# Running sums in the result's PSUM bank: a change to the seven-product steps of an attention and MLP kernel

## The chip, the cores and the metric

The kernel runs on one core of one Trainium2 chip. The metric is the device time of one execution in microseconds (us); lower is better. Three runs of the kernel before took 652.58, 654.79 and 655.5 us, median 654.79 us.

## The reference

A lightning attention (4 batches, 8 heads, 768 positions, head size 64) gives a token matrix `x` of 3072 x 512. An MLP follows:

```python
h = x @ w_in             # 3072x512 @ 512x2048
g = h - np.tanh(h)
return g @ w_out         # 3072x2048 @ 2048x512
```

The attention goes over blocks of positions with a running state per head (`kv_state`); scores inside a block are masked by powers of `lam`.

## The kernel before, in words

The tokens are worked off in six groups `g` = 0 to 5 of 512 tokens (128 positions of each batch). Each group passes attention, "up" (`x @ w_in` and the tanh step) and "down" (`g @ w_out`). Both products use Strassen's scheme in Winograd's form: a 2 x 2 block product is made of seven products P1 to P7 instead of eight, and sums of blocks are formed before and after. Groups 2 to 5 use the scheme on two levels: each of the seven outer products `n` is itself made of seven inner products `x`. On the inner level the results are, with P for the inner products:

- c11 = P1 + P2
- c12 = P1 + P6 + P5 + P3
- c21 = P1 + P6 + P7 + P4 (the signs are in the operands)
- c22 = P1 + P6 + P7 + P5

So three running sums are wanted, P1, P1 + P6 and P1 + P6 + P7. TensorE makes them in one place, `y`: P1 starts it, P6, P7 and P4 are added to it, and after each of them ScalarE copies the state of `y` away (line 819). P2 and P3 go to `zw`, where VectorE later picks them up.

`down_twice(g, n)` (from line 801) is an inner round of "down". Its inner product is 128 x 128, of four matrix products over the 2048 hidden units; each of the four appears in the trace as two passes, so an inner product is eight passes of TensorE. There are 32 calls: 5 in group 1 (n = 4, 5, 6, 7, 3), 7 in each of groups 2 to 4, and 6 in group 5. Each is a generator that hands control back after each inner product, and `steps` and `every` drive it. `y` is a part of one bank of PSUM (128 columns of 512), `zw` is a whole bank with P2, P3 and P5 in three quarters of it. VectorE adds P5 and P2 (lines 828 and 829), and then combines the outer products (lines 832 to 844). The rounds for n = 1 are woven into "up", those for n = 3 into `inner_steps`; all others (n = 2, 4, 5, 6, 7) run with their seven inner products one after the other.

`inner_steps(g, n)` (from line 627) is the same for "up" with n = 1, 2, 5, 6. Here two rounds run in turn, `pa` with `pb` (and with `down_twice` for n = 3 between them), then `pc` with `pd`. Each inner product is 128 x 512, of four products to four quarters of a bank.

`sums_twice` (lines 791 to 799) forms the sums of blocks that P5, P6, P7 and P3 read (`s1`, `s2`, `s3`, `s4`) on VectorE; for n > 2 `s4` is `a12 - s2`, in place of `a12`, once P2 has read `a12` (line 821). `sums_once` (line 743) forms operands of the outer level.

The weight blocks come from HBM through `send` on GpSimd's queue (line 700), seven ahead of their use (`RING`); the order of `stream` decides which is fetched first. `SUB` is the order in which they lie in HBM, `STEPS` that of their use.

PSUM has eight banks: `ya`, `yb`, `z`, `w` are single ones, `att` is a ring of four. A tile framework puts in the semaphores, one counter for each engine; it also orders instructions where `tied` and `keep_in_program_order` leave it free to.

After "down" n = 2 and after n = 6 comes `att_out` of the next group, small matrix products for the attention, whose results ScalarE copies to `xt` (line 484).

Of the kernel before, what the change touches and what calls it, by code (L numbers as in the profile page):

```python
# [15 lines left out]
AF = mybir.ActivationFunctionType  # L16
AL = mybir.AluOpType
# [7 lines left out]
def kernel(  # L25
# [32 lines left out]
    nc = tc.nc  # L58
# [6 lines left out]
    NG = S // BLK  # L65
    HB = GRP // 2
    NU = DFF // 512
# [61 lines left out]
    def tied(yes, op):  # L129
        return tc.keep_in_program_order(op) if yes else op  # L130
# [81 lines left out]
    SUB = (1, 2, 6, 5, 7, 3, 4)  # L212
    GI = 2
# [408 lines left out]
                nc.vector.tensor_tensor(dst, x, y, op=AL.subtract)  # L622
            toks[g, n] = {1: b11, 2: b21, 3: b22, 4: t4, 5: t1, 6: t2, 7: b12}

    STEPS = (1, 2, 6, 5, 7, 3, 4)

    def inner_steps(g, n):

        tags = {1: ("yb", "att", "att"), 2: ("w", "att", "att"), 5: ("ya", "att", "z"), 6: ("yb", "att", "att")}[n]
        y, w, z = (bank(x, tag, 4 if tag == "att" else 1) for x, tag in zip(("y3", "w3", "z3"), tags))  # L630
        r5 = otile("r5")
        out4 = hidden(g, {1: 12, 2: 11, 5: 22, 6: 21}[n])
        c11, c12, c21, c22 = (out4[:, :, i, ts(j, 128)] for i in range(2) for j in range(2))
        for x in STEPS:
            b = toks[g, n][x]
            wb = piece(g, ("in", n), x) if x in (3, 5, 6) else None
            dst = w if x == 2 else z if x in (3, 5) else y
            for u in range(NU):
                a = wb.rearrange("p m c -> p (m c)")[:, ts(u, 128)] if wb is not None else a_quarter(
                    n, u, *{1: (0, 0), 2: (0, 1), 7: (1, 0), 4: (1, 1)}[x])  # L640
                nc.tensor.matmul(out=dst[:, ts(u, 128)], lhsT=a, rhs=b, start=x in (1, 2, 5) and u == 0, stop=True,  # L641
                                 skip_group_check=True)
            d = dst.rearrange("q (u c) -> q u c", u=NU)
            if x in (1, 4, 6):
                op = tied(False, nc.scalar.activation({1: c11, 4: c21, 6: c12}[x], d, AF.Copy))  # L645
                if (n, x) == (1, 6) and g < NG - 1:
                    hold[g + 1] = op
                    load((g + 1) * B + 1)
            elif x == 5:
                tied(False, nc.scalar.activation(r5, dst, AF.Copy))  # L650
            elif x == 7:
                nc.vector.tensor_tensor(c22, r5.rearrange("q (u c) -> q u c", u=NU), d, op=AL.add)
            else:
                c = c11 if x == 2 else c12
                nc.vector.tensor_tensor(c, c, d, op=AL.add)
            yield
# [6 lines left out]
    def twice(g, n):  # L663
        return n in TWICE and not (g == NG - 1 and n == 3) and not (g < GI and n < 3)

    def pieces_of(g):
        for n in (1, 2, 4, 5, 6, 7):
            yield from ((g, n, x) for x in (SUB if twice(g, n) else range(NU)))
        if g == NG - 1:
            yield from ((g, 3, x) for x in range(NU))  # L670
            return
        for x in STEPS:
            yield g, 3, x
            if x in (3, 5, 6):
                yield from ((g + 1, ("in", n), x) for n in (1, 2))
        yield from ((g + 1, ("in", n), x) for x in STEPS if x in (3, 5, 6) for n in (5, 6))

# [1 line left out]
    sent = {"n": 0}  # L679

    EXTRA = 4
    rests = [stream.index((g, 5, x)) for g in range(1, NG) for x in SUB[:EXTRA]]
    rank = [i - sum(r < i for r in rests) for i in range(len(stream))]

    def send(i):
# [49 lines left out]
    res, low = {}, {}  # L735

    def sums_once(g, dst, x, y):

        for u in range(NU):
            sum_once(g, u, dst, x, y)  # L740
# [50 lines left out]
    def sums_twice(g, n):  # L791
        a11, a12, a21, a22 = quarter(g, n)

        s1, s2, s3, s4 = ([late["pool"].tile([128, NU, 128], F32, name=f"s{x}", tag="sums", bufs=6)
                           for x in range(1, 5 if n < 3 else 3)] + [a21, a12])[:4]
        for dst, x, y, op in ((s1, a21, a22, AL.add), (s2, s1, a11, AL.subtract), (s3, a11, a21, AL.subtract),
                              (s4, a12, s2, AL.subtract))[:4 if n < 3 else 3]:
            tied(n in (5, 3, 1, 2) or (g, n) == (1, 6), nc.vector.tensor_tensor(dst, x, y, op=op))  # L798
        low[g, n] = (s1, s2, s3, s4)

    def down_twice(g, n):
        a11, a12, a21, a22 = quarter(g, n)
        s1, s2, s3, s4 = low.pop((g, n))
        y, zw = (("ya", "z") if n in (4, 6) else ("yb", "w")) if g == NG - 1 else ("ya", "z") if n in (5, 3) else ("yb", "w")
        if n < 3:
            y, zw = "att", "w" if n == 2 else "att"
        y, zw = (bank(x, tag, 4 if tag == "att" else 1) for x, tag in (("y2", y), ("zw", zw)))
        y = y[:, 0:128]
        o = res[g, n] = otile(f"q{n}") if n != 2 else late["pool"].tile([128, 512], F32, name="o11", tag="o11", bufs=1)
        for x, a, dst, keep in ((1, a11, y, o[:, 0:128]), (2, a12, zw[:, 0:128], None), (6, s2, y, o[:, 128:256]),  # L810
                                (5, s1, zw[:, 256:384], None), (7, s3, y, o[:, 384:512]), (3, s4, zw[:, 128:256], None),
                                (4, a22, y, o[:, 256:384])):
            wb = piece(g, n, x).rearrange("p m c -> p (m c)")
            for u in range(NU):
                tied(x == STEPS[-1], nc.tensor.matmul(out=dst, lhsT=a[:, u, :], rhs=wb[:, ts(u, 128)],  # L815
                                                      start=x in (1, 2) and u == 0, stop=u == NU - 1,
                                                      skip_group_check=True))
            if keep is not None:
                nc.scalar.activation(keep, dst, AF.Copy)  # L819
            if x == 2 and n > 2:  # L820
                tied(n in (5, 7), nc.vector.tensor_tensor(a12, a12, s2, op=AL.subtract))  # L821
            if x != STEPS[-1]:
                yield

        if n in (6, 2):
            yield
        o5 = o.rearrange("q (i c) -> q i c", i=2)[:, :, 128:256]
        tied(n in (6, 2), nc.vector.tensor_tensor(o5, o5, zw[:, 256:384][:, None, :].to_broadcast([128, 2, 128]), op=AL.add))
        tied(n in (6, 2), nc.vector.tensor_tensor(o[:, 0:256], o[:, 0:256], zw[:, 0:256], op=AL.add))
        if n == 6:  # L830
            yield
            tc.keep_in_program_order(nc.vector.tensor_tensor(o, o, res[g, 1], op=AL.add))
            for x in (4, 5):
                tc.keep_in_program_order(nc.vector.tensor_tensor(res[g, x], res[g, x], o, op=AL.add))
        elif n == 2:
            tc.keep_in_program_order(nc.vector.tensor_tensor(o, o, res[g, 1], op=AL.add))
            store(g, 11, o)
        elif n == 7:
            nc.vector.tensor_tensor(res[g, 4], res[g, 4], o, op=AL.add)
            store(g, 21, res[g, 4])  # L840
            nc.vector.tensor_tensor(o, o, res[g, 5], op=AL.add)
            store(g, 22, o)
        elif n == 3:
            nc.vector.tensor_tensor(o, o, res[g, 5], op=AL.add)
            store(g, 12, o)
        yield

    def every(steps):
        for _ in steps:
            pass  # L850
# [84 lines left out]
    def steps(it, n):  # L935
        for _ in range(n):
            next(it)
# [94 lines left out]
    for g in range(1, NG):  # L1032
# [47 lines left out]
        else:  # L1080
# [1 line left out]
            sums_once(g, 11, "S1", 11)  # L1082
            p2 = down_twice(g, 2)
            steps(p2, len(STEPS))
        send(stream.index((g, 4, SUB[0])))
        if not last and g < GI:
            att_decays(g + 1, (0, 1))
        if not last:
            att_out(g + 1, (0, 1))
        every(p2)  # L1090
        if g >= GI:
            sums_twice(g, 5)
        p4 = down_twice(g, 4)
        if g == GI - 1:
            inner_weights(NU - 1, INNER[:2])
            steps(p4, 4)
# [2 lines left out]
        p5 = down_twice(g, 5)  # L1099
        if not last:  # L1100
            att_transpose(g + 1, (2,))
        steps(p5, 2)
        if not last:
            att_transpose(g + 1, (3,))
        steps(p5, 1)
        sums_once(g, 21, 21, 11)
        sums_twice(g, 6)
        every(p5)
        if not last:
            att_decays(g + 1, (2, 3))  # L1110
        if twice(g, 7):
            sums_twice(g, 7)
        p6, p7 = down_twice(g, 6), down_twice(g, 7)
        steps(p6, len(STEPS) + 1)
        if not last:
            att_out(g + 1, (2, 3))
        every(p6)
        steps(p7, 2)
        if not last:
            att_sums(g + 1, None)  # L1120
        every(p7)
        if last:
            down_end(g)
            continue
        inner_tokens(g + 1, INNER[:3])
        sums_twice(g, 3)
        p3, pa, pb, pc, pd = (down_twice(g, 3), *(inner_steps(g + 1, n) for n in INNER))
        for i, _ in enumerate(STEPS):
            next(p3)
# [49 lines left out]
```

## Time and profile before

| | us |
|---|---|
| profiled execution, its own time | 651.28 |
| its span, first to last instruction | 649.5 |
| three other runs | 652.58, 654.79, 655.5 (median 654.79) |
| TensorE (PE) busy | 641.2 of the span |
| VectorE (DVE) busy | 518.5 |
| ScalarE (ACT) busy | 249.2 |
| GpSimd (POOL) busy, with its DMA issues | 252.7 |

The profile shows one execution. PE rows are matrix products, PEld rows are weight loads that run beside them. Busy time of PE counts each pass from its start to its modelled end, and passes overlap, so it can't be read as use of the peak. "Idle before" is the time that an engine sat idle ahead of an instruction, with what ended it.

### The profile page before, as it was taken

The page shows a single profiled execution, that of the slowest core. Times are in us where ns is not written, and L with a number is a line of the kernel's source. Part 1 is how long each engine was busy: PE and PEld are TensorE (multiplying, and loading weights), DVE is VectorE, ACT ScalarE, POOL GpSimd, SP SyncE. Part 2 cuts the span into 40 slices and gives each one's busy share as a digit, 9 for nine tenths or more (in the row PEclk, how much of TensorE's full clock was granted, in tenths as well). Part 3 has the DMA queues.
Part 4 walks back from the last instruction along what each step waited for, and adds up shares of the span by engine and source line. Part 5 has one row for each costly group of instructions (what it writes and reads, how often), then busy time and mean ns, then how long its engine had stood idle before and what let it go on. Part 6 is the DMA issues. An engine that isn't in the chain of part 4 may idle for free.

```text
span 649.5 us, 16022 instructions
## 1 busy us (share of the span) xinstructions
PE 641.2 (99%) x6176; PEld 595.1 (92%) x6176; DVE 518.5 (80%) x1029; ACT 249.2 (38%) x513; POOL 252.7 (39%) x434
## 2 busy tenths in 40 slices
PE   8999999999999999999999999999999999999998
PEld 7888888888888999989999989999999999998997
DVE  4467989968999897699986679998479997479873
ACT  3685776513322222543223444213454223254210
POOL 6000126768756436404335312443422355421341
PEclk9999999999999999999999999999999999999999
DMA  9969986979979858968856987776986776731574
GB/s 202 223 167 202 256 259 227 369 239 262 258 181 271 250 175 274 242 150 212 267 172 216 237 169 187 234 242 196 246 180 133 239 258 218 232 124 36 185 249 164
DMA packets 161499, 139.75 MB, mean 215 GB/s; under 512 B 128896, under 2 KB 131200, under 8 KB 161424
## 3 DMA queue, kind: packets, MB, share of 16 engines
q0 software_dynamic: 31712, 101.81, 48.9%
q1 hardware_dynamic: 128096, 36.53, 27.0%
q8 instruction: 49, 0.80, 0.5%
q10 hardware_dynamic: 1616, 0.39, 0.4%
q14 instruction: 26, 0.21, 0.1%
HBM read 113.25 MB, written 25.43 MB: 214 GB/s over the span
## 4 chain that ended last, share of the span: by engine, by line
PE 71%; DVE 13%; DMA 7%; SPq 3%; issue 3%; ACT 2%; POOL 0%; DVEq 0%; ACTq 0%; POOLq 0%
PE y L815 13%; PE zw L815 10%; PE y L554 9%; PE y L641 7%; PE h L874 6%; PE z L554 5%; PE acc L904 4%; PE z L641 3%; SPq L171 3%; DMA k_blk<-in_k_dram 2%; DMA k_nat<-in_k_dram 2%; PE w L641 2%; DVE s L798 2%; DMA q_blk<-in_q_dram 2%; DVE g L563 2%
## 5 line engine op out<-in xcount | busy, mean ns | idle before, releaser
L700 POOL DMA_DIRECT2D wb<-fine x204 | 110.4, 542 | 221.0 <-PE y L815 163.2
L819 ACT ACTIVATE q<-y 128x128 f32<-128x128 f32 x112 | 31.1, 277 | 143.7 <-PE y L815 142.3
L815 PE MATMUL y<-wb,g 128*128 128x128 f32 x584 | 77.1, 277 | 0.0
L815 PEld LDWEIGHTS y<-wb,g 128*128 128x128 f32 x584 | 70.8, 192 | 0.9
L874 PE MATMUL h<-xt,w 128*128 128x256 f32 x256 | 57.8, 382 | 0.4 <-DVE w L325 0.4
L874 PEld LDWEIGHTS h<-xt,w 128*128 128x128 f32 x256 | 47.6, 190 | 7.8 <-DVE w L325 1.1
L815 PE MATMUL zw<-wb,g 128*128 128x128 f32 x368 | 48.9, 276 | 0.6 <-DVE g L821 0.6
L815 PEld LDWEIGHTS zw<-wb,g 128*128 128x128 f32 x368 | 44.8, 192 | 1.1 <-DVE g L821 1.0
L554 PE MATMUL y<-xt,w 128*128 128x256 f32 x192 | 45.4, 382 | 0.0
L562 ACT ACTIVATE th<-g 128x512 f32<-128x512 f32 x40 | 25.1, 628 | 47.4 <-DVE g L580 29.8
L554 PEld LDWEIGHTS y<-xt,w 128*128 128x128 f32 x192 | 35.5, 190 | 5.6 <-ACT y L529 1.1
L645 ACT ACTIVATE g<-y 128x512 f32<-128x512 f32 x48 | 28.6, 595 | 30.9 <-PE y L641 30.9
L554 PE MATMUL y<-tt,w 128*128 128x256 f32 x160 | 38.4, 382 | 0.0
L554 PE MATMUL z<-xt,ws 128*128 128x256 f32 x160 | 38.4, 382 | 0.0
L815 PE MATMUL zw<-wb,s 128*128 128x128 f32 x280 | 38.1, 276 | 0.2 <-DMA wb<-fine 0.2
L815 PE MATMUL y<-wb,s 128*128 128x128 f32 x280 | 38.1, 277 | 0.2
L815 PEld LDWEIGHTS y<-wb,s 128*128 128x128 f32 x280 | 35.1, 192 | 1.6 <-issue 0.7
L697 POOL DMA_DIRECT2D wb<-fine_in x48 | 25.9, 542 | 26.1 <-PE zw L815 9.5
L815 PEld LDWEIGHTS zw<-wb,s 128*128 128x128 f32 x280 | 34.8, 192 | 0.8 <-DVE s L798 0.6
L554 PEld LDWEIGHTS z<-xt,ws 128*128 128x128 f32 x160 | 30.1, 190 | 4.6 <-ACT z L529 0.7
L563 DVE TENSOR_TENSOR g<-g,th 128x512 f32<-128x512 f32 x40 | 27.2, 687 | 8.7 <-ACT th L562 8.2
L554 PEld LDWEIGHTS y<-tt,w 128*128 128x128 f32 x160 | 29.5, 190 | 4.8 <-DVE g L575 1.3
(220 smaller groups left out, 1497.2 us busy)
## 6 DMA issues: line engine op xcount, KB each, us to landing
wb<-fine POOLq DMA_DIRECT2D x204, 256.0 KB, 3.8
wb<-fine_in POOLq DMA_DIRECT2D x48, 256.0 KB, 4.1
raw<-in_moe_w_out_dram SPq DMA_DIRECT2D x12, 512.0 KB, 5.5
rest<-fine POOLq DMA_DIRECT2D x20, 256.0 KB, 4.8
raw<-in_moe_w_in_dram SPq DMA_DIRECT2D x16, 256.0 KB, 6.5
fine<-f POOLq DMA_DIRECT2D x16, 256.0 KB, 4.7
q_blk<-in_q_dram SPq DMA_DIRECT2D x128, 32.0 KB, 3.3
k_blk<-in_k_dram SPq DMA_DIRECT2D x128, 32.0 KB, 4.2
```

The costliest lines, as they stand in the source:

```text
L171: op = tc.keep_in_program_order(nc.sync.dma_start(out=x[ts(c, 32), :, r], in_=heads[c // 2, g * BLK + 32 * r:g * BLK + 32 * (r + 1), :, ts ...
L554: nc.tensor.matmul(out=t[:, m, :], lhsT=wt[:, kt, ts(m, 128)], rhs=x[:, kt, :], start=first and m == 0 and kt == 0, stop=kt == 1, skip_gro ...
L562: nc.scalar.activation(th, src, AF.Tanh)
L563: nc.vector.tensor_tensor(dst(c), src, th, op=AL.subtract)
L641: nc.tensor.matmul(out=dst[:, ts(u, 128)], lhsT=a, rhs=b, start=x in (1, 2, 5) and u == 0, stop=True, skip_group_check=True)
L645: op = tied(False, nc.scalar.activation({1: c11, 4: c21, 6: c12}[x], d, AF.Copy))
L697: nc.gpsimd.dma_start(out=t.rearrange("p m c -> p (m c)"), in_=fine_in[INNER.index(n_[1]), (5, 6, 3).index(x_)].rearrange("p u c -> p (u c)"))
L700: nc.gpsimd.dma_start(out=t.rearrange("p m c -> p (m c)"), in_=fine[TWICE.index(n_), SUB.index(x_)].rearrange("p u c -> p (u c)"))
L815: tied(x == STEPS[-1], nc.tensor.matmul(out=dst, lhsT=a[:, u, :], rhs=wb[:, ts(u, 128)], start=x in (1, 2) and u == 0, stop=u == NU - 1, s ...
L819: nc.scalar.activation(keep, dst, AF.Copy)
L874: tied(u == 0, nc.tensor.matmul(out=hm[c][:, m, :], lhsT=w1[u][:, i, a, ts(m, 128)], rhs=xt[0, t][:, i, :], start=m == 0 and i == 0, stop= ...
L904: nc.tensor.matmul(out=acc[n][:, r, :], lhsT=a[:, ts(r, 128)], rhs=b, start=kt == 0 and r == 0, stop=kt == KH - 1, skip_group_check=True)
```

## The change

Products go in the order 1, 5, 6, 2, 7, 3, 4 instead of 1, 2, 6, 5, 7, 3, 4. ScalarE's copies of the running sums now go into `zw` itself: the quarters of that bank are c11, c12, c21, c22. TensorE then adds P2 onto c11 and P3 onto c12, so no VectorE add is left for P2 and P3. P5 moves from `zw` to a second quarter of the bank of `y` and is copied by ScalarE to `r5` (in SBUF), and VectorE adds it to c12 and c22 in one instruction. For n = 1, 4, 5 the result is wanted in SBUF by itself (`alone`): P2 and P4 are then copied there, by one more ScalarE copy. For the other n VectorE's combining adds read `zw`. In "up" the same is done for n = 1, 5 and 6 (`seeded`): ScalarE copies P1 to `w`, P2 is added there, and ScalarE copies `w` away, where VectorE had added.

The in-place `a12 - s2` moves to after P6 and is written to `s2`. Some calls of `sums_twice` and `sums_once` stand a few inner products earlier or later, and the weight blocks are fetched in the new order.

```diff
-    STEPS = (1, 2, 6, 5, 7, 3, 4)
+    STEPS = (1, 5, 6, 2, 7, 3, 4)
...
-        tags = {1: ("yb", "att", "att"), 2: ("w", "att", "att"), 5: ("ya", "att", "z"), 6: ("yb", "att", "att")}[n]
+        tags = {1: ("att", "w", "att"), 2: ("yb", "att", "att"), 5: ("ya", "z", "att"), 6: ("yb", "w", "att")}[n]
+        seeded = tags[1] != "att"
...
             if x in (1, 4, 6):
-                op = tied(False, nc.scalar.activation({1: c11, 4: c21, 6: c12}[x], d, AF.Copy))
+                to = w.rearrange("q (u c) -> q u c", u=NU) if seeded and x == 1 else {1: c11, 4: c21, 6: c12}[x]
+                op = tied(False, nc.scalar.activation(to, d, AF.Copy))
...
+            elif x == 2 and seeded:
+                tied(False, nc.scalar.activation(c11, d, AF.Copy))
...
-        y = y[:, 0:128]
+        y, p5 = y[:, 0:128], y[:, 128:256]
+        c11, c12, c21, c22 = (zw[:, ts(x, 128)] for x in range(4))
+        alone = n in (1, 4, 5)
+        s4 = s4 or s2
...
-        for x, a, dst, keep in ((1, a11, y, o[:, 0:128]), (2, a12, zw[:, 0:128], None), (6, s2, y, o[:, 128:256]),
-                                (5, s1, zw[:, 256:384], None), (7, s3, y, o[:, 384:512]), (3, s4, zw[:, 128:256], None),
-                                (4, a22, y, o[:, 256:384])):
+        r5 = o[:, 384:512]
+        for x, a, dst, keep in ((1, a11, y, c11), (5, s1, p5, r5), (6, s2, y, c12),
+                                (2, a12, c11, o[:, 0:128] if alone else None), (7, s3, y, c22), (3, s4, c12, None),
+                                (4, a22, y, o[:, 256:384] if alone else c21)):
...
-                tied(x == STEPS[-1], nc.tensor.matmul(out=dst, lhsT=a[:, u, :], rhs=wb[:, ts(u, 128)],
-                                                      start=x in (1, 2) and u == 0, stop=u == NU - 1,
+                tied(x == STEPS[-1] or n > 1, nc.tensor.matmul(out=dst, lhsT=a[:, u, :], rhs=wb[:, ts(u, 128)],
+                                                      start=x == 1 and u == 0, stop=u == NU - 1,
...
             if keep is not None:
                 nc.scalar.activation(keep, dst, AF.Copy)
-            if x == 2 and n > 2:
-                tied(n in (5, 7), nc.vector.tensor_tensor(a12, a12, s2, op=AL.subtract))
+            if x == 6 and n > 2:
+                tied(n in (5, 7), nc.vector.tensor_tensor(s2, a12, s2, op=AL.subtract))
...
+        z5, o5 = (t.rearrange("q (i c) -> q i c", i=2)[:, :, 128:256] for t in (zw, o if alone else zw))
+        tied(n in (6, 2), nc.vector.tensor_tensor(o5, z5, r5[:, None, :].to_broadcast([128, 2, 128]), op=AL.add))
...
-        tied(n in (6, 2), nc.vector.tensor_tensor(o5, o5, zw[:, 256:384][:, None, :].to_broadcast([128, 2, 128]), op=AL.add))
-        tied(n in (6, 2), nc.vector.tensor_tensor(o[:, 0:256], o[:, 0:256], zw[:, 0:256], op=AL.add))
...
-            tc.keep_in_program_order(nc.vector.tensor_tensor(o, o, res[g, 1], op=AL.add))
+            tc.keep_in_program_order(nc.vector.tensor_tensor(o, zw, res[g, 1], op=AL.add))
```

More of the change, by code (lines that the diff above doesn't have):

```diff
@@ L640, in inner_steps @@
                     n, u, *{1: (0, 0), 2: (0, 1), 7: (1, 0), 4: (1, 1)}[x])
-                nc.tensor.matmul(out=dst[:, ts(u, 128)], lhsT=a, rhs=b, start=x in (1, 2, 5) and u == 0, stop=True,
-                                 skip_group_check=True)
+                tc.keep_in_program_order(nc.tensor.matmul(
+                    out=dst[:, ts(u, 128)], lhsT=a, rhs=b, start=(x in (1, 5) or x == 2 and not seeded) and u == 0,
+                    stop=True, skip_group_check=True))
             d = dst.rearrange("q (u c) -> q u c", u=NU)
             if x in (1, 4, 6):
-                op = tied(False, nc.scalar.activation({1: c11, 4: c21, 6: c12}[x], d, AF.Copy))
+                to = w.rearrange("q (u c) -> q u c", u=NU) if seeded and x == 1 else {1: c11, 4: c21, 6: c12}[x]
+                op = tied(False, nc.scalar.activation(to, d, AF.Copy))
                 if (n, x) == (1, 6) and g < NG - 1:
@@ L667, in pieces_of @@
         for n in (1, 2, 4, 5, 6, 7):
-            yield from ((g, n, x) for x in (SUB if twice(g, n) else range(NU)))
+            yield from ((g, n, x) for x in (STEPS if twice(g, n) else range(NU)))
         if g == NG - 1:
@@ L681 @@
     EXTRA = 4
-    rests = [stream.index((g, 5, x)) for g in range(1, NG) for x in SUB[:EXTRA]]
+    rests = [stream.index((g, 5, x)) for g in range(1, NG) for x in STEPS[:EXTRA]]
     rank = [i - sum(r < i for r in rests) for i in range(len(stream))]
@@ L794, in sums_twice @@
         s1, s2, s3, s4 = ([late["pool"].tile([128, NU, 128], F32, name=f"s{x}", tag="sums", bufs=6)
-                           for x in range(1, 5 if n < 3 else 3)] + [a21, a12])[:4]
+                           for x in range(1, 5 if n < 3 else 3)] + [a21, None])[:4]
         for dst, x, y, op in ((s1, a21, a22, AL.add), (s2, s1, a11, AL.subtract), (s3, a11, a21, AL.subtract),
@@ L819, in down_twice @@
                 nc.scalar.activation(keep, dst, AF.Copy)
-            if x == 2 and n > 2:
-                tied(n in (5, 7), nc.vector.tensor_tensor(a12, a12, s2, op=AL.subtract))
+            if x == 6 and n > 2:
+                tied(n in (5, 7), nc.vector.tensor_tensor(s2, a12, s2, op=AL.subtract))
             if x != STEPS[-1]:
                 yield
+        z5, o5 = (t.rearrange("q (i c) -> q i c", i=2)[:, :, 128:256] for t in (zw, o if alone else zw))
+        tied(n in (6, 2), nc.vector.tensor_tensor(o5, z5, r5[:, None, :].to_broadcast([128, 2, 128]), op=AL.add))
         if n in (6, 2):
             yield
-        o5 = o.rearrange("q (i c) -> q i c", i=2)[:, :, 128:256]
-        tied(n in (6, 2), nc.vector.tensor_tensor(o5, o5, zw[:, 256:384][:, None, :].to_broadcast([128, 2, 128]), op=AL.add))
-        tied(n in (6, 2), nc.vector.tensor_tensor(o[:, 0:256], o[:, 0:256], zw[:, 0:256], op=AL.add))
         if n == 6:
             yield
-            tc.keep_in_program_order(nc.vector.tensor_tensor(o, o, res[g, 1], op=AL.add))
+            tc.keep_in_program_order(nc.vector.tensor_tensor(o, zw, res[g, 1], op=AL.add))
             for x in (4, 5):
@@ L835, in down_twice @@
         elif n == 2:
-            tc.keep_in_program_order(nc.vector.tensor_tensor(o, o, res[g, 1], op=AL.add))
+            tc.keep_in_program_order(nc.vector.tensor_tensor(o, zw, res[g, 1], op=AL.add))
             store(g, 11, o)
         elif n == 7:
-            nc.vector.tensor_tensor(res[g, 4], res[g, 4], o, op=AL.add)
+            nc.vector.tensor_tensor(res[g, 4], res[g, 4], zw, op=AL.add)
             store(g, 21, res[g, 4])
-            nc.vector.tensor_tensor(o, o, res[g, 5], op=AL.add)
+            nc.vector.tensor_tensor(o, zw, res[g, 5], op=AL.add)
             store(g, 22, o)
         elif n == 3:
-            nc.vector.tensor_tensor(o, o, res[g, 5], op=AL.add)
+            nc.vector.tensor_tensor(o, zw, res[g, 5], op=AL.add)
             store(g, 12, o)
@@ L1084 @@
             steps(p2, len(STEPS))
-        send(stream.index((g, 4, SUB[0])))
+        send(stream.index((g, 4, STEPS[0])))
         if not last and g < GI:
@@ L1090 @@
         every(p2)
+        p4 = down_twice(g, 4)
         if g >= GI:
             sums_twice(g, 5)
-        p4 = down_twice(g, 4)
+            steps(p4, 3)
+            sums_once(g, 21, 21, 11)
         if g == GI - 1:
@@ L1101 @@
             att_transpose(g + 1, (2,))
-        steps(p5, 2)
+        steps(p5, 3)
         if not last:
             att_transpose(g + 1, (3,))
-        steps(p5, 1)
-        sums_once(g, 21, 21, 11)
+        if g < GI:
+            sums_once(g, 21, 21, 11)
         sums_twice(g, 6)
@@ L1110 @@
             att_decays(g + 1, (2, 3))
-        if twice(g, 7):
-            sums_twice(g, 7)
         p6, p7 = down_twice(g, 6), down_twice(g, 7)
-        steps(p6, len(STEPS) + 1)
+        steps(p6, 3)
+        sums_twice(g, 7)
+        steps(p6, len(STEPS) - 2)
         if not last:
@@ L1119 @@
         if not last:
+            sums_twice(g, 3)
+            steps(p7, 1)
             att_sums(g + 1, None)
@@ L1125 @@
         inner_tokens(g + 1, INNER[:3])
-        sums_twice(g, 3)
         p3, pa, pb, pc, pd = (down_twice(g, 3), *(inner_steps(g + 1, n) for n in INNER))
```

## The prediction

> **What bounds the kernel now.** I read the page first: busy times, the granted clock, the chain, the costliest groups.
>
> ```profile
> PE 641.2 (99%) x6176; PEld 595.1 (92%) x6176; DVE 518.5 (80%) x1029; ACT 249.2 (38%) x513; POOL 252.7 (39%) x434
> ...
> PEclk9999999999999999999999999999999999999999
> ...
> PE 71%; DVE 13%; DMA 7%; SPq 3%; issue 3%; ACT 2%; POOL 0%; DVEq 0%; ACTq 0%; POOLq 0%
> ...
> L819 ACT ACTIVATE q<-y 128x128 f32<-128x128 f32 x112 | 31.1, 277 | 143.7 <-PE y L815 142.3
> L815 PE MATMUL y<-wb,g 128*128 128x128 f32 x584 | 77.1, 277 | 0.0
> ```
>
> TensorE sets the time: 71% of the chain, no idle time ahead of the largest group of the inner rounds, clock at nine tenths or more in every slice. ScalarE is the opposite: it waits for TensorE 142 us in total before its copies of `y`. So work put on ScalarE is cheap as work. What matters is whether TensorE then waits for ScalarE.
>
> The next view is the timeline of one inner round of `down_twice` (group 1, n = 4). Columns: start, length (of all x8 passes together), engine, line, operation, out<-in.
>
> ```profile
> 212.37 1.16 PE L815 MATMUL y<-wb,g 128*128 128x128 f32 x8
> ...
> 213.37 1.06 PE L815 MATMUL zw<-wb,g 128*128 128x128 f32 x8
> ...
> 213.57 0.28 ACT L819 ACTIVATE q<-y 128x128 f32<-128x128 f32 x1
> ...
> 214.26 1.06 PE L815 MATMUL y<-wb,s 128*128 128x128 f32 x8
> ```
>
> P1 into `y`, P2 into `zw`, P6 into `y` again. Between P2 and P6 lie 0.89 us for eight passes, 0.11 us each. P1's last pass starts at 213.37 - 0.11 = 213.26; the copy starts 0.31 us after that and ends at 213.85, 0.59 us after it. P6 adds to `y` and must come after the copy; it starts at 214.26, 0.41 us later. That is why the copies cost nothing now: **P2 stands between a product of `y` and the next, and its 0.89 us is longer than the copy's round trip.** P5 does the same between P6 and P7, and P3 between P7 and P4.
>
> **What the change does to TensorE's order.** No product is added or removed (3120 in both programs). But the built program's waits show what covers what. This is one round of the changed kernel (group 1, n = 7; the first matrix product of each of products 5, 6, 2, 7, 3):
>
> ```
> 580 L828 Matmult y_2529<-wb,s_2377 128x128 [waits DMASW3_49,Activation_49]
> 582 L828 Matmult y_2529<-wb,s_2378 128x128 [waits DMASW4_49,Activation_49]
> 584 L828 Matmult zw<-wb,g_1575 128x128 [waits DMASW5_49,DVE_49,Activation_49]
> 586 L828 Matmult y_2529<-wb,g_1575 128x128 [waits DMASW6_49]
> 588 L828 Matmult zw<-wb,s_2378 128x128 [waits DMASW7_49,DVE_49,Activation_49]
> ```
>
> By the value of the counter, P5 waits for the copy of P1, P6 for that of P5, P2 for that of P6, P3 for that of P7: each for a copy of the product straight before it. P5 writes other columns than the copy reads, but the same bank; P2 adds to c11 while the copy of P6 writes c12, the same bank again. In such a place nothing lies between. Counted over the program: before, no product of line 815 waits for a copy with nothing between, and 7 with less than a whole product. In the changed one 94 have nothing between, and 5 half a product (0.45 us). The 24 rounds that aren't woven into other work (4 in group 1, 5 in each of groups 2, 3, 4 and 5) have four each, 96, of which 2 fall under the half products. The other 3 are in the rounds n = 1.
>
> The Trainium skill ("PSUM — Partial Sum Buffer", section on bank collisions) says that accesses of two engines to PSUM are to be kept apart by bank and quadrant, not by address. By it the waits above are needed; guarded by address alone there would be none, and the time would be that of the last rival below. No product in the trace of before writes a bank under a copy, so it can't tell.
>
> **What such a wait costs.** The nearest row is a product that waits for VectorE:
>
> ```profile
> 228.74 1.16 PE L815 MATMUL y<-wb,g 128*128 128x128 f32 x8
> ...
> 229.80 0.68 DVE L821 TENSOR_TENSOR g<-g,s 128x512 f32<-128x512 f32 x1
> ...
> 230.54 0.97 PEld L815 LDWEIGHTS zw<-wb,g 128*128 128x128 f32 x8 [0.83 <-DVE g L821]
> 230.54 1.16 PE L815 MATMUL zw<-wb,g 128*128 128x128 f32 x8 [0.64 <-DVE g L821]
> ...
> 231.53 0.72 PE L815 MATMUL y<-wb,g 128*128 128x128 f32 x5
> ```
>
> VectorE ends at 230.48, the weight load starts 0.05 to 0.06 us later: it was not pulled ahead of the wait. The next product starts at 231.53, after 0.99 us instead of 0.89: a first pass after a pause costs 0.10 more. So from the start of the last pass: 0.31 to the copy, 0.28 copy, 0.05 to the load: 0.64. Without a wait the next pass starts after 0.11. Pause 0.53, plus 0.10: **0.63 us each.**
>
> Two of the four copies (P6's, P7's) write a bank that ScalarE wrote just before, so the program gives them two waits, and the one for TensorE stands in an instruction of its own. The trace of before has that form too:
>
> ```profile
> 244.78 1.61 PE L641 MATMUL y<-xt,w 128*128 128x128 f32 x13
> 245.03 0.28 ACT L819 ACTIVATE q<-y 128x128 f32<-128x128 f32 x1 [0.66 <-PE y L815]
> ```
>
> Here the copy starts 0.25 us after the following product, not 0.20 as at 213.57: 0.05 more, so 0.68. Three of the four copies go to PSUM instead of SBUF; for 128x512 the rows are 581 ns (`w<-y`, line 529) against 595 (`g<-y`, line 645), so 0.015 less. A round: 0.63 + 0.63 + 0.68 + 0.68 - 0.05 = 2.57 us, on 7 x 0.89 = 6.2.
>
> - 24 rounds x 2.57 = 61.7 us.
> - Two of these pauses in the last round have a half product in them: -0.9. Three more in n = 1: 0.68 - 0.45 each, +0.7. Sum 61.5.
>
> **What else moves.**
> - VectorE loses 32 adds of 128x256 (417 ns each, line 829) and 12 of 128x512 (682 ns, line 655): 13.3 + 8.2 = 21.5 us. ScalarE gains 46 copies of 0.28 and 12 of 0.6: 20 us, on an engine that is 62% idle. Neither is on the path but through waits of TensorE for VectorE. Those are small: ahead of the weight loads of line 815 stand 0.9, 1.1, 1.6 and 0.8 us in the four large groups, 4.4 in all. A pause for ScalarE lets VectorE catch up, so some of this vanishes: the parts named for VectorE, 1.0 + 0.6, and 0.3 us in three groups where `att_out` waits for the scores' masks (line 393). I take -2.5, bounds 0 and -4.4.
> - `a12 - s2` (0.69 us) now waits for P6 rather than P2; P3 needs it. Between lie P2, P7 and two pauses, 3.1 us (before: three products, 2.7). Nothing; without that cover, 0.69 a round. Queued behind it on VectorE are sums for later rounds, which the longer round gives more time.
> - Copies of P1 in n = 4 and 7 come behind `xt` copies, and for n = 4 and 7 also behind the VectorE add that still reads the bank of the round before, because it is now `zw` and not `o` that this add reads. At 341.59 the copy started 0.25 us after the following product, 0.05 late. The add stands right behind line 482 on VectorE, which P1 itself waits for. Nothing; a whole activation in the way would be 0.6 each.
> - In `inner_steps` each product waits for a copy with at least one other product of 0.89 us between, mostly two. The round trip of its 128x512 copy is 0.31 + 0.60 + 0.05 - 0.11 = 0.85. Covered, barely at 4 places.
> - DMA: the same transfers on the same queues, the weight blocks in the new order. SP's and POOL's queues hold as many, and TensorE asks for blocks later. Nothing.
>
> Sum: 61.5 - 2.5 = +59. Against the profiled execution, 651.28, that is 710.3. It was the fastest of the four executions shown, whose mean is 653.5, so I predict 712.
>
> **Range.** Low: 0.53 for a pause (no slow first pass), 94 x 0.53 = 50, less 4.4, on 651.3: 697. High: 0.68 for each, 64, and in the 12 rounds that follow other ScalarE work (n = 2, 4, 7) one activation of 0.6 ahead of the first copy, 7, on the slowest run, 655.5: 726.5. I open it to 695 to 727.
>
> **Rivals.**
> - *The clock falls.* With a pause of 0.6 us after four products of seven, the clock could be taken back in these rounds. The first passes of the trace are 0.21 us apart (14 passes in 3.19 us at 1.65 us), against 0.11. At that rate 24 rounds x 56 passes x 0.10 = 134 us more: about 845. Against it: from 12 to 16 us TensorE was busy 3.31 of 4.0 us, with a wait of 0.69 at 13.05, and the granted clock in that window is 1.00. 5%. The Trainium skill ("TensorE: Matmul & The Clock Gate", second HAM failure mode) tells of such frequent small pauses bringing the clock to oscillate; by it this case would come true, and no run here shows it.
> - *Part of the pauses was waiting before, in a form that these rows don't show.* From 316 to 334.6 VectorE is busy 18.26 of 18.60 us; if the rounds were paced by it, half of the pauses would take the place of VectorE's lag: 653.5 + 30 = 683. Against it: TensorE's eight passes come every 0.89 us there with no gap. 4%.
> - *Faster.* The 21.5 us off VectorE free TensorE of its waits, and the new waits are met when they are reached. It turns on whether a copy ends within 0.11 us of the last pass's start, or 94 pauses stay under 4.4 / 94 = 0.05 us each. Then 653.5 - 4.4 = 649. The row at 213.57 gives 0.59 instead of 0.11. 2%.
> - *The change's waits don't bite* (other products slip in between, or the waits go by address): gain and loss under 3 us, 653. The order printed above is the engine's own. 2%.
>
> **Chances.** The forecast 87%, the rivals 5, 4, 2 and 2. A measurement of this kernel tells about 0.5%, 3.3 us, from no change. Slower by more: 96%; within it: 2%; faster: 2%.
>
> **What would show it.** In the profile after: PE idle time ahead of line 828 of about 50 us (the pauses without their slow first pass), ended by ACT line 832, in 90 or more places of 0.5 to 0.6 us; rounds of 8.8 us instead of 6.2; line 832 with 174 copies; ACT and issue on the chain where it was PE; VectorE's busy time some 22 us lower; "up" from 245 to 300 us as long as before. The step is wrong if products after such a wait start within 0.2 us of the last pass, if the pauses are much longer than 0.7 (another activation ahead of the copies), or if passes inside a product come at other than 0.11 us.

## The result, and the profile after

| | before | after |
|---|---|---|
| median of six runs, us | 655.14 (652.58 to 657.26) | 712.38 (709.76 to 714.2) |
| profiled execution, its own time / its span, us | 651.28 / 649.5 | 709.76 / 708.0 |

The ratio is 1.0874, with a 95% interval of 1.0841 to 1.0908: the changed kernel is slower by 57 us.

First the page of the changed kernel: busy times, the granted clock, the chain, and two of the costliest groups (busy and mean ns of one, then the idle time ahead of the group and what ended it).

```profile
PE 664.0 (94%) x6176; PEld 600.2 (85%) x6176; DVE 503.6 (71%) x985; ACT 264.6 (37%) x571; POOL 252.9 (36%) x434
...
PEclk9999999999999999999999999999999999999999
...
PE 88%; ACT 5%; DVE 3%; issue 2%; DMA 2%; ACTq 0%; DVEq 0%
...
L832 ACT ACTIVATE zw<-y 128x128 f32<-128x128 f32 x114 | 29.9, 262 | 143.8 <-PE y L828 142.7
...
L828 PEld LDWEIGHTS zw<-wb,s 128*128 128x128 f32 x256 | 31.3, 191 | 14.4 <-ACT zw L832 14.2
```

TensorE has as many instructions as before, at the same clock, and the span is 58.5 us longer. Weight loads that had no idle time ahead of them now wait for ScalarE's line 832. How often, the view of waits says (us in total, times, longest):

```profile
PE zw L828 <- ACT zw L832: 18.9, 46, 0.4
PE y L828 <- ACT zw L832: 9.4, 24, 0.7
PE y L828 <- ACT q L832: 7.3, 20, 0.4
PE y L828 <- ACT o L832: 1.5, 4, 0.4
...
PEld zw L828 <- ACT zw L832: 29.2, 51, 0.6
PEld y L828 <- ACT zw L832: 13.9, 24, 0.8
PEld y L828 <- ACT q L832: 11.1, 20, 0.6
PEld y L828 <- ACT o L832: 2.2, 4, 0.6
```

The products wait in 46 + 24 + 20 + 4 = 94 places and the weight loads in 99. These are the 94 waits with nothing between and the 5 with half a product that the prediction counted in the built program. The two totals, 37.1 us and 56.4 us, are the same pauses seen in two ways: a product counts as busy until its modelled end, 0.16 us after the next one would have started, so a pause of 0.53 us shows as 0.37 of idle time on PE. From start to start, and beyond the 0.11 us of a pass, the 94 pauses hold 52.4 us, and the slow pass behind each another 9.5.

The timeline of the round n = 4 of group 1, the one that the prediction showed for the kernel before (start, length of the x8 passes together, engine, line, operation, idle time and what ended it):

```profile
212.41 1.16 PE L828 MATMUL y<-wb,g 128*128 128x128 f32 x8
213.60 0.26 ACT L832 ACTIVATE zw<-y 128x128 f32<-128x128 f32 x1
213.91 1.16 PE L828 MATMUL y<-wb,s 128*128 128x128 f32 x8 [0.35 <-ACT zw L832]
215.11 0.28 ACT L832 ACTIVATE q<-y 128x128 f32<-128x128 f32 x1 [1.25 <-PE y L828]
215.44 1.16 PE L828 MATMUL y<-wb,s 128*128 128x128 f32 x8 [0.37 <-ACT q L832]
217.01 1.16 PE L828 MATMUL zw<-wb,g 128*128 128x128 f32 x8 [0.41 <-ACT zw L832]
218.00 1.06 PE L828 MATMUL y<-wb,g 128*128 128x128 f32 x8
219.47 1.16 PE L828 MATMUL zw<-wb,s 128*128 128x128 f32 x8 [0.41 <-ACT zw L832]
```

P1, then P5, P6 and P2, each after a pause, then P7 without one, and P3 after a pause. A product and the next start 0.89 us apart where nothing lies between (P2 has 0.99, for its slow first pass) and 1.47 to 1.57 where the next must wait for a copy. P5 writes columns 128 to 255 of the bank of `y`, the copy at 213.60 reads columns 0 to 127 of it: P5 starts 0.05 us after the copy's end. The next two rounds start at 221.36 and 230.21, 8.85 us apart.

### The profile page after: what moved, and what is told of

It is laid out like the page before. It is cut to its first block, busy times and chain, and to the rows that moved or that the text cites. A ratio compares the mean times of both kernels' runs of the same rounds, so it can differ in the third digit from the quotient of the medians.

```text
span 708.0 us, 16052 instructions
## 1 busy us (share of the span) xinstructions
PE 664.0 (94%) x6176; PEld 600.2 (85%) x6176; DVE 503.6 (71%) x985; ACT 264.6 (37%) x571; POOL 252.9 (36%) x434
## 4 chain that ended last, share of the span: by engine, by line
PE 88%; ACT 5%; DVE 3%; issue 2%; DMA 2%; ACTq 0%; DVEq 0%
PE y L828 22%; PE y L554 12%; PE zw L828 10%; PE y L644 8%; PE h L886 7%; PE z L554 6%; PE z L644 4%; PE acc L916 4%; ACT zw L832 3%; PE w L644 2%; PE op L462 2%; PE sp L387 2%; PE kv L408 1%; PE op L433 1%; PE op L473 1%
## 5 line engine op out<-in xcount | busy, mean ns | idle before, releaser
L832 ACT ACTIVATE zw<-y 128x128 f32<-128x128 f32 x114 | 29.9, 262 | 143.8 <-PE y L828 142.7
L828 PE MATMUL y<-wb,s 128*128 128x128 f32 x496 | 69.8, 283 | 14.6 <-ACT zw L832 7.6
L828 PEld LDWEIGHTS y<-wb,s 128*128 128x128 f32 x496 | 61.5, 191 | 22.6 <-ACT zw L832 11.2
L828 PE MATMUL zw<-wb,s 128*128 128x128 f32 x256 | 36.2, 285 | 9.4 <-ACT zw L832 9.4
L828 PEld LDWEIGHTS zw<-wb,s 128*128 128x128 f32 x256 | 31.3, 191 | 14.4 <-ACT zw L832 14.2
L562 ACT ACTIVATE th<-g 128x512 f32<-128x512 f32 x40 | 25.1, 628 | 45.6 <-DVE g L580 29.4
L828 PE MATMUL zw<-wb,g 128*128 128x128 f32 x216 | 30.8, 285 | 7.4 <-ACT zw L832 7.4
L834 DVE TENSOR_TENSOR s<-g,s 128x512 f32<-128x512 f32 x19 | 13.1, 690 | 34.1 <-PE y L828 34.0
L828 PEld LDWEIGHTS zw<-wb,g 128*128 128x128 f32 x216 | 26.2, 191 | 12.1 <-ACT zw L832 11.9
L916 PE MATMUL acc<-wt,g 128*128 128x256 f32 x144 | 33.5, 382 | 0.4 <-DVE g L922 0.2
```

The source lines that it names most:

```text
L562: nc.scalar.activation(th, src, AF.Tanh)
L828: tied(x == STEPS[-1] or n > 1, nc.tensor.matmul(out=dst, lhsT=a[:, u, :], rhs=wb[:, ts(u, 128)], start=x == 1 and u == 0, stop=u == NU - ...
L834: tied(n in (5, 7), nc.vector.tensor_tensor(s2, a12, s2, op=AL.subtract))
L916: nc.tensor.matmul(out=acc[n][:, r, :], lhsT=a[:, ts(r, 128)], rhs=b, start=kt == 0 and r == 0, stop=kt == KH - 1, skip_group_check=True)
```

## Experiments

Seven kernels. The theory: the loss is the 94 round trips from a product to ScalarE's copy and back, with nothing to lie under them, and TensorE waits because two parts of one bank are in use, not because it needs the data. The rivals: the new order itself, the mere number and destination of the copies, and the queue of ScalarE's other work. The line of the inner products is 816, 822, 828, 829, 831 or 832 in these kernels, that of the copies 820, 826, 833, 835 or 836. The kernel before took 654.33 us (median) beside the first four and 653.78 beside the other three, but 655.14 beside the changed kernel, so differences from the changed kernel's 712.38 carry an uncertainty of about 1 us.

**The order alone.** The kernel before with the products of "down" and the weight blocks in the new order, and `a12 - s2` after P6 and into `s2`; copies and VectorE's adds stay as before.

```diff
-    STEPS = (1, 2, 6, 5, 7, 3, 4)
+    STEPS = (1, 5, 6, 2, 7, 3, 4)
...
-        for x, a, dst, keep in ((1, a11, y, o[:, 0:128]), (2, a12, zw[:, 0:128], None), (6, s2, y, o[:, 128:256]),
-                                (5, s1, zw[:, 256:384], None), (7, s3, y, o[:, 384:512]), (3, s4, zw[:, 128:256], None),
+        for x, a, dst, keep in ((1, a11, y, o[:, 0:128]), (5, s1, zw[:, 256:384], None), (6, s2, y, o[:, 128:256]),
+                                (2, a12, zw[:, 0:128], None), (7, s3, y, o[:, 384:512]), (3, s4, zw[:, 128:256], None),
```

> The kernel before with the new order 1, 5, 6, 2, 7, 3, 4 alone (with the weight blocks fetched in that order and a12 - s2 made after P6); P5 stays in zw, the running sums are copied to SBUF, VectorE adds P2 and P3 as before. Theory (the pauses come from waits for a copy of the product straight before, in the same bank): no product waits for a copy with less than a whole product between, so the time is that of the kernel before, 655 us, within 3. Rival A (the order itself costs: sums on VectorE are needed earlier, P5 second instead of fourth): a good part of the 57 us is there already, 670 to 710.

Measured: 658.44 us, ratio 1.0064 (1.0043 to 1.0085). No pause for a copy. But it is 4.1 us slower than before, a little past what was expected, and the trace has most of it in line 816, where VectorE is late:

```profile
PE zw L816 <- DVE s L822: 2.1, 5, 0.8
...
528.92 0.68 DVE L822 TENSOR_TENSOR s<-g,s 128x512 f32<-128x512 f32 x1
529.66 0.71 PE L816 MATMUL zw<-wb,s 128*128 128x128 f32 x4 [0.80 <-DVE s L822]
```

Six times P3 waits for `a12 - s2`, 3.1 us in all from start to start, and five times P5 for the sum that it reads (four of them in n = 2), 2.9 us. The profiled execution also has 2.9 us of idle time ahead of line 473 (0.4 before), and the profile does not name what ended it; that part stays open. So of the change's 57 us the order by itself explains 4. Nor is it simply part of them: in the changed kernel these two waits are gone but for 0.3 us in each of two places, since the pauses for ScalarE give VectorE the time.

**The order and "up".** The same with `inner_steps` as changed. In this kernel P1 is left out of part of c11 in the seeded rounds, as read off the program's `start` flags; it has the 12 VectorE instructions less and the 12 ScalarE instructions more that were meant.

```diff
+                to = w.rearrange("q (u c) -> q u c", u=NU) if seeded and x == 1 else {1: c11, 4: c21, 6: c12}[x]
...
+            elif x == 2 and seeded:
+                tied(False, nc.scalar.activation(c11, d, AF.Copy))
```

> The order as in the run above, and the seeded form for up's P1, P5 and P6 (12 VectorE adds less, 12 ScalarE copies more); down as before. Theory: every product of up has a product of the other round between itself and the copy that it waits for, 0.89 us against a round trip of 0.85, so no change: 655 us, within 3, perhaps 1 less by the 8 us taken off VectorE. Rival B (a ScalarE write into a PSUM bank that TensorE adds to is dear by itself, with or without cover): 12 such places, up to 8 us more, 660 or more.

Measured: 660.87 us, ratio 1.0103 (1.0076 to 1.013), 2.4 us more than the order alone. The two intervals overlap, but the time is outside the theory's range and past 660, where rival B began. The traces speak against rival B: from the first to the last pass the products of `inner_steps` take 31.3 us in the first group and 30.3 in each of the other three, with the order alone 30.9 and 30.3, so 12 copies into a bank that TensorE adds to do not cost 8 us there. In four places, one a group, a weight load waits 0.06 us for a copy with one product between. What the profile has more lies scattered (0.55 us at the products of "up", 2 at the scores). So "up" costs little, and whether it costs anything stays open.

**One of the four waits, and no more copies.** The order alone, with P5 moved to the second quarter of the bank of `y`, where VectorE reads it at the end. Nothing is copied more often and nothing is copied to PSUM: all that is new is that P5 shares a bank with the P1 that ScalarE is reading.

```diff
-        y = y[:, 0:128]
+        y, p5 = y[:, 0:128], y[:, 128:256]
...
-        for x, a, dst, keep in ((1, a11, y, o[:, 0:128]), (5, s1, zw[:, 256:384], None), (6, s2, y, o[:, 128:256]),
+        for x, a, dst, keep in ((1, a11, y, o[:, 0:128]), (5, s1, p5, None), (6, s2, y, o[:, 128:256]),
...
-                                                      start=x in (1, 5) and u == 0, stop=u == NU - 1,
+                                                      start=x in (1, 2) and u == 0, stop=u == NU - 1,
```

> The order run, with one thing more: P5 goes to the second quarter of the bank of y instead of to zw, and VectorE reads it there at the end. No ScalarE copy is added or moved. P5 then waits for the copy of P1, in 24 places with nothing between. Theory: 24 pauses of 0.63 us, +15 us: 670 us (668 to 673), and in the trace 24 pauses of 0.53 us ahead of P5, each with a slow first pass. Rival B (the copies, or their number, cost): no copy more than before, so 655 us.

Measured: 676.82 us, ratio 1.0355 (1.0323 to 1.0387): 18.4 us more than the order alone and 3.8 us above the expected range. From the waits and the timeline of the profiled execution (681.05 us, the slowest of the four):

```profile
PEld y L816 <- ACT q L820: 12.5, 20, 1.8
...
PE sp L387 <- DVE ss L393: 3.6, 3, 1.4
...
217.25 0.28 ACT L820 ACTIVATE q<-y 128x128 f32<-128x128 f32 x1
217.59 2.05 PE L816 MATMUL y<-wb,s 128*128 128x128 f32 x16 [0.37 <-ACT q L820]
```

P5 and P6 run as sixteen passes without a gap, and ahead of P5 stands the same pause as in the changed kernel, in 24 places: 0.53 us in 16 of them, 0.58 in four, where the copy has a wait instruction of its own, and 0.10 for the pass behind it. At 0.63 each the 24 are the 15 us of the expectation. The other four are longer: three times 0.72 to 0.92 us, where VectorE's sum for P5 came after the copy, and once 1.74 us, where the copy itself waited for VectorE (at 663.14). This kernel alone also has three waits at the scores of the next group, 4.3 us in all. They fit a bank of the ring that stays taken until VectorE has added P5; I have not tested that by a run. A wait of TensorE on a copy that touches none of its columns costs what the sum said.

**Two of the four waits taken away.** The changed kernel, but with P5 in a bank of its own for n = 2, 4, 5, 6 and 7. It makes the same copies with the same sizes.

```diff
-        y, p5 = y[:, 0:128], y[:, 128:256]
+        own = n not in (1, 3)
+        y, p5 = y[:, 0:128], bank("p5", "att", 4)[:, 128:256] if own else y[:, 128:256]
...
-                                                      start=x == 1 and u == 0, stop=u == NU - 1,
+                                                      start=(x == 1 or own and x == 5) and u == 0, stop=u == NU - 1,
```

> The changed kernel, but P5 of the rounds n = 2, 4, 5, 6, 7 gets a bank of its own from the ring of four. Same products, copies and adds. P5 then waits for no copy and P6 only for that of P1, with P5 between; P2 and P3 still wait for the copies of P6 and P7 into their bank. Theory: 47 of the 94 pauses are left, those of 0.66 us; 24 x (0.62 + 0.63) = 30 us less than the changed kernel: 682 us (679 to 686). Rival B (the 58 copies more, or copies into PSUM): nothing changes, 712 us.

Measured: 685.12 us, ratio 1.0473 (1.0453 to 1.0493), 27.3 us less than the changed kernel. The timeline of the round that was shown above:

```profile
214.61 1.16 PE L829 MATMUL y<-wb,g 128*128 128x128 f32 x8
215.61 1.06 PE L829 MATMUL p<-wb,s 128*128 128x128 f32 x8
216.50 1.06 PE L829 MATMUL y<-wb,s 128*128 128x128 f32 x8
217.97 1.16 PE L829 MATMUL zw<-wb,g 128*128 128x128 f32 x8 [0.41 <-ACT zw L833]
```

P1, P5 and P6 follow each other 0.89 to 1.00 us apart, without a pause for a copy; P2 still pauses, and P3. 47 pauses are left, each of 0.574 us, those for the bank of `zw`. The 48 ahead of P5 and P6 are gone, which held 31 us with their slow passes, and one ahead of P2 is new. Some 3 us come back as VectorE's lag (P5 of n = 2 waits up to 0.77 us for its sum, P6 0.26), as in the order alone.

**Something to lie between.** The changed kernel with the rounds n = 4 and 5 in turn, inner product by inner product, so that a product of the other round stands in each of their pauses.

```diff
+        p4, p5 = down_twice(g, 4), down_twice(g, 5)
+        for i in range(len(STEPS)):
+            next(p4)
+            next(p5)
...
+        yield from ((g, n, x) for x in STEPS for n in (4, 5))
```

> The changed kernel, with the rounds n = 4 and n = 5 run in turn, an inner product of the one and then of the other (their banks differ; the weight blocks are fetched in that order). Same products, copies and adds. Each copy of these 10 rounds then has a product of 0.89 us between itself and the product that waits for it, against a round trip of 0.53. Theory: 40 pauses of 0.64 us go, 54 stay: 712.4 - 25.7 = 687 (684 to 690; up to 3 of it VectorE's lag, which the pauses hid). Rival B (the 58 copies more, or copies into PSUM): no change, 712.

Measured: 693.92 us, ratio 1.0607 (1.058 to 1.0633): 18.5 us less than the changed kernel, but 4 us above the range that was expected. The 54 places are left that were expected. Pauses and gaps in line 831 are 22 us less than in line 828 of the changed kernel. The turn-taking brings losses of its own; the largest one:

```profile
231.43 0.42 DVE L842 TENSOR_TENSOR q<-zw,q 128x256 f32<-128x256 f32 x1
...
231.94 0.26 ACT L835 ACTIVATE zw<-y 128x128 f32<-128x128 f32 x1 [3.17 <-DVE q L842]
...
232.26 0.94 PE L831 MATMUL y<-wb,s 128*128 128x128 f32 x6 [2.91 <-ACT zw L835]
```

Here the copy of P1 cannot go into the bank for `zw` until VectorE has added what the round before left there, and TensorE waits 3.07 us for both. The kernel before had no such link, since its copies went to SBUF. Two waits of 1.16 and 1.38 us of `zw` behind "up" and 1.4 at the end for a weight block come with it; together some 6 of the 7 us that are missing. I have not separated these by a run. (A wait of 2.3 us in line 462 stands at 26.4 us, before the first of these rounds, so the turns do not cause it.)

**Both cures.** Rounds 4 and 5 in turn, and P5 in a bank of its own for n = 2, 6 and 7.

> Both cures together: n = 4 and 5 in turn, and P5 of n = 2, 6 and 7 in a bank of its own. 27 places are left with nothing between (P2 and P3 of 14 rounds, less one). Theory: 27 x 0.67 = 18 us over the order-only run's 658.4, less what the pauses hide of VectorE's lag (0 to 4): 674 (671 to 678). Rival B: no change, 712.

Measured: 677.38 us, ratio 1.0348 (1.0328 to 1.0368), as expected: 27 pauses of 0.574 us are left, and VectorE's lag has grown to 4.5 us ahead of P5, 2.4 of it in one place. The two waits for `zw` behind "up" are there too, 1.20 and 1.32 us.

**The copies twice as long.** The changed kernel with each copy of P1, P5, P6 and P7 issued twice in a row. If the waits were a fixed cost of the order or of the bank, doubling would change little; if TensorE stands still for the copy, each pause grows by one copy.

```diff
-                nc.scalar.activation(keep, dst, AF.Copy)
+                for _ in range(2 if x in (1, 5, 6, 7) else 1):
+                    nc.scalar.activation(keep, dst, AF.Copy)
```

> The changed kernel with each of the copies of P1, P5, P6 and P7 in down's inner rounds made twice in a row, into the same place (128 more ScalarE copies). If a pause is the round trip to ScalarE and back, each of the 94 grows by one copy and the wait of the second for the first, 0.28 to 0.36 us, and the covered ones do not: 712.4 + 26 to 34, 742 (738 to 747). If a pause is a fixed cost of the bank (TensorE held off for a set time after another engine's access), nothing or little is added: 712 to 718.

Measured: 737.77 us, ratio 1.1284 (1.1257 to 1.1312), 25.4 us more than the changed kernel.

```profile
215.17 0.56 ACT L833 ACTIVATE zw<-y 128x128 f32<-128x128 f32 x2
215.78 1.16 PE L828 MATMUL y<-wb,s 128*128 128x128 f32 x8 [0.65 <-ACT zw L833]
216.97 0.59 ACT L833 ACTIVATE q<-y 128x128 f32<-128x128 f32 x2 [1.25 <-PE y L828]
217.61 1.16 PE L828 MATMUL y<-wb,s 128*128 128x128 f32 x8 [0.68 <-ACT q L833]
```

The idle times of 0.35 and 0.37 have become 0.65 and 0.68: a copy more, to a hundredth of a microsecond. From start to start the pauses went from 0.514 to 0.808 (P5), 0.530 to 0.839 (P6) and 0.574 to 0.867 us (P3). Only P2's grew by less, 0.574 to 0.807; over its 23 places that is 1.4 us, more than the 0.2 us by which the time came out below the range. In this kernel line 833 has 93 separate wait instructions on ScalarE, where line 832 had 121; the copy of P6 starts 1.20 us after P6's first pass, where it was 1.26. ScalarE's busy time rose by 33 us, and the kernel became slower by that part of it that has no product above it.

Put together (time, and the pauses for a copy with nothing between):

| kernel | pauses | us |
|---|---|---|
| order and "up" | 0 | 660.87 |
| P5 in the bank of `y` | 24 | 676.82 |
| both cures | 27 | 677.38 |
| P5 in its own bank | 47 | 685.12 |
| rounds in turn | 54 | 693.92 |
| changed kernel | 94 | 712.38 |
| the same, each pause a copy longer | 94 | 737.77 |

From the first row to the changed kernel a pause is worth 51.5 / 94 = 0.55 us. That fits its 0.615 to 0.675 less the lag of VectorE, some 6 us, which the first row has and the pauses hide. No version came below the kernel before, and none of these points to one: TensorE has no idle time there that a shorter list of adds on VectorE could give back, but for the 4 us of VectorE's waits.

## Why the prediction was right, point by point

- *Where the bound is.* Right: TensorE's stream, now with ScalarE's copies in it. VectorE's instructions add up to 20.9 us less, against 21.5 counted; its busy time, in which overlapping instructions count once, fell by 14.9 (518.5 to 503.6). Neither bought more than the 4 us below.
- *94 waits with nothing between, 5 with half a product.* Right to the place: 94 and 99 in the two views of waits.
- *The price of one.* Right: pauses of 0.514 (P5; 0.563 in 7 places, where its copy too has a wait instruction of its own), 0.530 (P6) and 0.574 us (P2, P3), and 0.101 for the slow first pass, 0.615 to 0.675 together. The 0.05 for the separate wait instruction is there to see in the 0.574, and so is the shorter copy to PSUM (262 ns against 278). In two groups P5 of n = 2 waits 0.82 instead of 0.51. The view names ScalarE there, but when P5 starts at 314.14 the copy had ended 0.36 us before, and VectorE's sum, which P5 reads, only 0.10 before: a remnant of the lag that the order alone shows. ScalarE was not late there, as the upper bound allowed. A round was to take 8.8 us and takes 8.85. The 94 pauses with their slow passes: 61.9 us, and some 0.8 for the five with half a product, against 61.5 for both.
- *That the wait goes by bank.* Right, for this program: P5's pause is there with P5 in the bank of `y` (two kernels) and gone with it in another (two kernels). It is the program that holds TensorE back; whether the memory itself would have allowed the two accesses was not tried, as the two would race. This is also where the Trainium skill's rule on bank collisions ("PSUM — Partial Sum Buffer") led to the right count.
- *VectorE's waits returned, -2.5.* Inside its bounds, but more came back: 2.0 us in these rounds and 2.1 in line 462, about half of which had been waits for the scores' masks. Against that, one wait of 1.0 us for VectorE at the very end is new.
- *`a12 - s2` costs nothing.* Right, and for the reason given, the two pauses: without them, in the order alone, it costs 3.1 us.
- *"Up" and DMA cost nothing.* The products of `inner_steps` take 30.3 us a group before (line 641) and 30.3 to 30.5 after (line 644), those of line 554 25.0 and 25.0 to 25.1 in groups 2 to 5. The four places that were called barely covered are there: a weight load 0.06 us late in each group. By time, "up" costs at most the 2.4 us of the second experiment, if that is not noise.
- *The rivals.* The clock stayed at 1.00 with 94 pauses of 0.51 to 0.57 us, four in each round and 1.5 to 3.3 us apart, so the 845 us did not come. The oscillation from frequent small pauses of which the Trainium skill tells ("TensorE: Matmul & The Clock Gate", second HAM failure mode) did not arise here. The VectorE lag that half of the pauses were to replace (683 us) is the 6.0 us that the order alone uncovers, not 30. The faster case needed copies that end within 0.11 us of the last pass; they end after 0.57 to 0.64.
- *The 712 itself.* That it came within 0.4 us is in part luck: the sum was +59 on a base of 653.5, and measured were +57.2 on 655.14.

Three of the signs were wrong in size or kind. VectorE's busy time was to be some 22 us lower and is 14.9 lower. The idle time ahead of line 828 was to be about 50 us; PE shows 37.1, since a busy product hides 0.16 us of each pause, and the weight loads 56.4. And ScalarE and issue were to take PE's place on the chain: ScalarE went from 2 to 5%, but PE rose from 71 to 88% and VectorE fell from 13 to 3%. The chain follows what released each step, and with VectorE rarely late it runs along PE.

## What to carry to other kernels

Where the program guards PSUM by bank, as here, a copy of a running sum is free only as long as enough work stands between it and the next access to its bank: here one whole product, 0.89 us against the pause of 0.51 to 0.57. Before reordering an accumulation, list for each product the last wait and what lies between, and price those with nothing between at (last pass to copy + copy + release - one pass + slow first pass), here 0.62 to 0.68 us. Taking work off an engine that only rarely ends a wait gains no more than those waits, here 4 us for 21 us of instructions.

## What the runs showed of the hardware that was not expected

- The pauses are constant: 0.513 or 0.514, 0.529 to 0.531, 0.563 or 0.573 or 0.574 us, with the two exceptions of 0.82, in all groups of the program. Such a price, read off once, can be multiplied.
- A busy share can rise with the loss: PE is 22.8 us busier in the changed kernel with the same 6176 products, for the slow passes and the modelled ends that now stand alone.
- The clock was not taken back in any of the kernels with pauses; the mean granted clock was between 0.997 and 1.0 in every profiled execution.
